# Modulation weights in three chunks instead of four, the last two by narrow strips, with the dummy products on a built-in constant

## The chip, the cores and the metric

The kernel runs on one core of a Trainium2 chip. The metric is the device time of one execution in microseconds (us), and the number that counts is the median of several runs. A profiled execution of the same program, taken by the hardware profiler, gives the trace that the prediction reads.

## What is computed

One block of a two-stream (image and text) transformer with adaptive layer norm: B = 2 batches, 256 image and 32 text tokens each, width D = 1152, all in bfloat16. Cut to the image side, which is what the change touches:

```python
mod = silu(c) @ wmod_img                      # [B, 6*D]; parts 0, 1, 2 are shift, scale, gate
h   = layernorm(x_img) * (1 + scale) + shift
q, k, v = split(h @ wqkv_img)                 # the text side does the same with its own weights
p   = softmax(concat(q_t, q) @ concat(k_t, k).T * D**-0.5)
out = x_img + gate * ((p @ concat(v_t, v)) @ wo_img)
```

## The kernel before, in words

The width of 1152 is KT = 9 blocks of P = 128. The 512 image tokens are four x tiles of 128 rows (tiles 0 and 1 are batch 0, tiles 2 and 3 batch 1). The program is one hand-written order (`manual_schedule`, L62): every engine carries out its instructions in the order of the source, and waits only on semaphores.

**Loads.** All weights come through one queue on SP, in the order of the source. x tiles 0 and 1 go by ACT's queue (L100). On SP there follow the scale weights `w_sc_i` and the value weights `w_v_i` in turn: `KC` (L49) cuts the nine blocks into the chunks 0-1, 2-3, 4-5 and 6-8; `load_sc` (L92) fetches a chunk of scale weights (rows of 512 bytes for two blocks, of 768 bytes for three), `load_v` (L96) the value weights of the same blocks, one block of 288 KB at a time (rows of 2304 bytes). x tile 2 comes behind the first scale chunk, x tile 3 behind value block 6, and then value blocks 7 and 8 in one transfer (L109). After that come the shift weights (`w_sh_i`) and the query weights (`w_q_i`), in thirds.

**Warm-up.** `warm` (L140) issues dummy products of 512 columns on a tile `wz`, which VectorE (DVE) has set to zero (L124): four, then the transpose of `c` and the SiLU (`silu_c`), then eleven more (L312).

**Layer norm and scale.** DVE normalises an x tile into `xn_i` (`stats_of`, `std_of`, `out_of`, L317; the square root is ACT's, L176). TensorE (PE) transposes its blocks: the first H = 2 as "heads" (`x_heads`, L198), which ACT writes out already multiplied by the scale (`head_scaled`, L205), and the others as "tails" (`x_tails`, L210), which are copied out plain (`tail_out`, L217) and multiplied later (`apply_mod`, L251). The scale itself comes in two ways. `mod_scale` (L226) makes it with 9 products of two columns for each block, so 18 for a chunk, and it lands in the layout in which it is used. `mod_scale_last` (L235), used for the last chunk, makes a strip: 4 opening products, 36 products of 96 columns in four column groups of the array, and a 32x32 transpose by DVE (L248) that turns it into columns.

**Values.** `v_row(i, kt)` (L297) multiplies block kt of x tile i with 2 x 512 columns of value weights ("wide" products, L282), `v_narrow` (L290) with the last 128. Seven accumulators stay open over all nine blocks, so these run block by block as chunks arrive (L346 to L402). x tile 3 comes last: `last_transposes` (L301) makes all nine blocks, DVE multiplies them by the scale, and `v_wide(3, ...)` follows. Then comes a strip for the shift (`mod_strip`, L429) and, from L534 on, the query products (L529) and the rest of the block.

Of the kernel before, what the change touches and what calls it, by code (L numbers as in the profile page):

```python
# [8 lines left out]
ACT = mybir.ActivationFunctionType  # L9
# [5 lines left out]
def kernel(  # L15
# [14 lines left out]
    nc = tc.nc  # L30
# [6 lines left out]
    P = 128  # L37
# [8 lines left out]
    SCALE = float(D) ** -0.5  # L46
    EPS = 1e-5

    KC = [(0, 2), (2, 4), (4, 6), (6, KT)]  # L49
    VW = 512  # L50
    NM = 1024

# [52 lines left out]
    for ch in range(1, len(KC)):  # L105
        load_sc(ch)
        if ch < len(KC) - 1:
            load_v(ch)
    for k0, k1 in ((6, 7), (7, KT)):  # L109
        nc.sync.dma_start(w_v_i[:, k0:k1, :], w_view(wqkv_img)[:, k0:k1, 2 * D:3 * D])  # L110
        if k1 < KT:
            load_x(3)
    K3 = ((0, 3), (3, 6), (6, KT))
    K2 = ((0, 5), (5, KT))
    w_sh_i = load_w(wmod_img, 0, K3)
# [5 lines left out]
    eps_t = const.tile([P, 1], f32)  # L121
    nc.vector.memset(eps_t[:], EPS)
    nc.gpsimd.memset(x_t[:], 0.0)
    wz = const.tile([P, VW], bf)  # L124
    nc.vector.memset(wz[:], 0.0)  # L125
    sT32 = const.tile([P, KT, 32], bf)
    nc.gpsimd.memset(sT32[:], 0.0)
    ones_full = const.tile([P, B * 32 + 96], bf)
# [8 lines left out]
    sTw = sTw_full[:, 0:KT * NT].rearrange("p (k b t) -> p k b t", k=KT, b=B)  # L137


    def warm(n):  # L140
        for _ in range(n):
            ps = ps_mm.tile([P, VW], f32, tag="mm", name="wps")
            nc.tensor.matmul(ps[:], lhsT=wz[:, 0:P], rhs=wz[:], start=True, stop=True)  # L143

    sT = const.tile([P, KT, B], bf)

# [55 lines left out]
            nc.tensor.transpose(tp[:, kt, :], xn_i[:, i, kt * P:(kt + 1) * P], ident[:])  # L202
        return tp

    def head_scaled(tp, i):  # L205
        for kt in range(H):
            nc.scalar.activation(hT_i[:, kt, i * P:(i + 1) * P], tp[:, kt, :], ACT.Identity,
                                 scale=mod_i[:, kt, i // TPB:i // TPB + 1])

    def x_tails(i):  # L210
        pool, tag = (ps_mm, "mm") if i < TPB else (ps_sm, "sm")
        tp = pool.tile([P, KT - H, P], bf, tag=tag, name="tp")
        for kt in range(H, KT):
            nc.tensor.transpose(tp[:, kt - H, :], xn_i[:, i, kt * P:(kt + 1) * P], ident[:])
        return tp
# [7 lines left out]
                nc.tensor.matmul(out_ps[:, j - j0, :], lhsT=wt[:, kt, j * P:(j + 1) * P], rhs=sT[:, kt, :],  # L223
                                 start=(kt == 0), stop=(kt == KT - 1))

    def mod_scale(ch, eng, pool=ps_sm, tag="sm"):  # L226
        k0, k1 = KC[ch]
        mps = pool.tile([P, KT, B], f32, tag=tag)
        mod_cols(w_sc_i, mps, k0, k1)
        if eng == "dve":  # L230
            nc.vector.tensor_scalar_add(mod_i[:, k0:k1, :], mps[:, 0:k1 - k0, :], 1.0)
        else:
            nc.scalar.activation(mod_i[:, k0:k1, :], mps[:, 0:k1 - k0, :], ACT.Identity, bias=1.0)

    def mod_scale_last():  # L235
        k0, k1 = KC[3]
        n = (k1 - k0) * 32
        gps = ps_sm.tile([P, n], f32, tag="sm", name="sps3")
        for g in range(NGG):
            nc.tensor.matmul(gps[32 * g:32 * g + 32, :], lhsT=unit[:, 0:32], rhs=unit[:, 0:n], start=True, stop=False,  # L240
                             tile_position=(0, 32 * g))
        for kt in range(KT):
            cols = w_sc_i[:, kt, k0 * P:k1 * P].rearrange("p (m g j) -> p g m j", m=k1 - k0, g=NGG)
            for g in range(NGG):
                nc.tensor.matmul(gps[32 * g:32 * g + 32, :], lhsT=sT32[:, kt, :], rhs=cols[:, g],
                                 start=False, stop=(kt == KT - 1), tile_position=(0, 32 * g))
        t = work.tile([P, VC + 32], f32, tag="of", bufs=1, name="scols")[:, 0:n]
        nc.vector.transpose(t, gps[:])  # L248
        scols[0] = t.rearrange("p (k r) -> p k r", r=32)[:, :, 0:B]

    def apply_mod(kt, t0, t1, shift, eng):  # L251
        b = t0 // TPB
        sl = hT_i[:, kt, t0 * P:t1 * P]
        if shift:
            ap = shift_i[:, kt, b:b + 1]
        elif kt >= KC[3][0]:
            ap = scols[0][:, kt - KC[3][0], b:b + 1]
        else:
            ap = mod_i[:, kt, b:b + 1]
        op = ALU.add if shift else ALU.mult  # L260
        if eng == 0:
            nc.vector.tensor_scalar(sl, sl, ap, None, op0=op)
        elif eng == 1:
            if shift:
                nc.gpsimd.tensor_scalar(sl, sl, 1.0, ap, op0=ALU.mult, op1=ALU.add)
            else:
                nc.gpsimd.tensor_scalar(sl, sl, ap, 0.0, op0=ALU.mult, op1=ALU.add)
        elif shift:
            nc.scalar.activation(sl, sl, ACT.Identity, bias=ap, scale=1.0)
        else:  # L270
            nc.scalar.activation(sl, sl, ACT.Identity, scale=ap)
# [37 lines left out]
            nc.vector.tensor_mul(hT_i[:, j0:j1, i * P:(i + 1) * P], tp[:, j0 - k0:j1 - k0, :],  # L309
                                 mod_i[:, j0:j1, b:b + 1].to_broadcast([P, j1 - j0, P]))  # L310

    warm(4)  # L312
    silu_c()
    warm(11)
    lns = {}

    def stats_of(i, k0, k1):  # L317
# [10 lines left out]
    stats_of(1, 0, NCH)  # L328
    std_of(1)
    out_of(0)  # L330
    mod_scale(0, "act")
    out_of(1)
    tails = []
    for i in range(TPB):
        heads = x_heads(i)
        tails.append(x_tails(i))
        head_scaled(heads, i)
    stats_of(2, 0, NCH)
    tail_out(0, tails[0], H, H + 3)
    std_of(2)  # L340
    tail_out(0, tails[0], H + 3, KT)
    tail_out(1, tails[1], H, H + 3, on_vector=True)
    out_of(2, 0, H * P)
    tail_out(1, tails[1], H + 3, KT, on_vector=True)
    out_of(2, H * P, D)
    for kt in range(*KC[0]):  # L346
        for i in range(TPB):
            v_row(i, kt)
    for i in range(TPB):
        v_narrow(i, *KC[0])  # L350
    head2 = x_heads(2)
    mod_scale(1, "dve")
    head_scaled(head2, 2)
    apply_mod(2, 0, 2, False, 0)
    apply_mod(3, 0, 2, False, 1)
    v_wide(2, 0, *KC[0])
    v_narrow(2, *KC[0])
    tail2 = x_tails(2)
    tail_out(2, tail2, H, KT)
    v_wide(2, 1, *KC[0])  # L360
    for kt in range(*KC[1]):
        apply_mod(kt, 2, 3, False, 0)
    for kt in range(*KC[1]):
        for i in range(TPB):
            v_row(i, kt)
    mod_scale(2, "dve")
    for kt in range(*KC[2]):
        apply_mod(kt, 0, 2, False, 0)
        apply_mod(kt, 2, 3, False, 1)
    for kt in range(*KC[1]):  # L370
        v_row(2, kt)
    k0, k1 = KC[2]
    for i in range(3):
        v_row(i, k0)
    for i in range(TPB):
        v_row(i, k0 + 1)
    for i in range(3):
        v_narrow(i, *KC[1])
    mod_scale_last()
    for n, kt in enumerate(range(*KC[3])):  # L380
        apply_mod(kt, 0, 2, False, (0, 1, 2)[n])
        apply_mod(kt, 2, 3, False, (2, 0, 1)[n])
    nc.gpsimd.tensor_copy(mod_i[:, KC[3][0]:KT, :], scols[0])
    v_row(2, k0 + 1)
    for i in range(3):
        v_narrow(i, k0, k1)
    stats_of(3, 0, NCH)
    std_of(3)
    out_of(3)
    k0 = KC[3][0]  # L390
    for i in range(3):
        v_row(i, k0)
        v_narrow(i, k0, k0 + 1)
    for i in range(3):
        for half in range(2):
            v_wide(i, half, k0 + 1, KT)
        v_narrow(i, k0 + 1, KT)
        if i == 1:
            last_transposes(0, KT - 1, ps_sm, "sm")
            last_transposes(KT - 1, KT, ps_mm, "mm")  # L400
    v_wide(3, 0, 0, KT)
    v_narrow(3, 0, KT)  # L402
# [58 lines left out]
    nc.sync.dma_start(x_t[0:P:P // NTT, :], xt_flat[:, :])  # L461
    w_q_t = load_w(wqkv_txt, 0, K2)
    w_k_t = load_w(wqkv_txt, D, K2)
    w_ga_i = load_w(wmod_img, 2 * D, K2, home="V")
    w_v_t = load_w(wqkv_txt, 2 * D, K3)
    w_o_i = load_w(wo_img, 0, K2)
    w_ga_t = load_w(wmod_txt, 2 * D)
# [461 lines left out]
```

## Time and profile before

| | us |
|---|---|
| median of 3 runs (114.64 to 114.8) | 114.69 |
| the profiled execution, its own time | 114.88 |
| its span, first to last instruction | 113.1 |
| PE busy in the span | 108.3 |
| DVE, ACT and POOL busy | 76.1, 36.6, 28.4 |

All times in the views count from the start of the span. The profiled execution took 1.8 us more than its span and 0.19 us more than the median. A line of a timeline has the start, the time from the first start to the last end, the engine, the source line, the operation, output and inputs, the count, and in brackets the idle time before it with what ended it. Products of PE overlap in the pipe, so the pace of a group is read from the start of one group to the start of the next. SPq and ACTq are the issues of transfers on these queues, not the transfers.

### The profile page before, as it was taken

How to read it: one execution, taken by the hardware profiler on the slowest of the kernel's cores; microseconds unless marked ns; L12 is line 12 of the kernel's file. 1: busy time of each engine (PE TensorE's matmuls, PEld its weight loads, DVE VectorE, ACT ScalarE, POOL GpSimd, SP SyncE). 2: the span in 40 equal slices, each digit the busy share in tenths (PEclk: the TensorE clock that was granted, in tenths of full speed). 3: DMA queues.
4: the chain of work that ended last, by engine and by line, in shares of the span. 5: the costliest groups of instructions: out<-in, count | busy, mean ns of one | idle time of the engine just before them, and what ended most of it. 6: DMA issues, size and time to landing. Idle time of an engine off the chain costs nothing.

```text
span 113.1 us, 2863 instructions
## 1 busy us (share of the span) xinstructions
PE 108.3 (96%) x1195; PEld 64.0 (57%) x1204; DVE 76.1 (67%) x151; ACT 36.6 (32%) x83; POOL 28.4 (25%) x65
## 2 busy tenths in 40 slices
PE   5999999999999999999999999999999999999990
PEld 1356655555444444444446558787687556567670
DVE  1699330956399999999999950237666802995971
ACT  4537500372190071740008924025646700001000
POOL 7100120730140000000000060601550470699300
PEclk9999999999999999999999999999999999999998
DMA  3999999999999999999999999999999999994052
GB/s 92 343 333 355 375 375 405 412 411 408 407 412 412 410 411 402 413 410 412 412 411 415 408 405 407 408 392 394 407 411 397 412 408 406 371 375 161 0 191 70
DMA packets 22839, 40.87 MB, mean 361 GB/s; under 512 B 1375, under 2 KB 6635, under 8 KB 22827
## 3 DMA queue, kind: packets, MB, share of 16 engines
q1 hardware_dynamic: 21547, 39.05, 90.4%
q10 hardware_dynamic: 672, 0.77, 2.2%
q0 software_dynamic: 608, 0.88, 2.1%
q8 instruction: 9, 0.15, 0.5%
q14 instruction: 3, 0.02, 0.1%
HBM read 39.36 MB, written 1.34 MB: 360 GB/s over the span
## 4 chain that ended last, share of the span: by engine, by line
PE 80%; DMA 13%; SPq 4%; issue 1%; DVE 0%
PE qkps L529 31%; PE ps L851 16%; DMA w_sc_i<-in_wmod_img_dram 13%; PE va L282 7%; PE aps L759 5%; PE ps L590 4%; PE sps L619 4%; PE gps L429 3%; SPq L98 3%; PE ops L869 2%; PE ps L694 2%; PE van L294 1%; PE gps L824 1%; PE sps L632 1%; PE pk L703 1%
## 5 line engine op out<-in xcount | busy, mean ns | idle before, releaser
L529 PE MATMUL qkps<-hT_i,t 128*128 128x512 bf16 x158 | 35.4, 379 | 0.2
L529 PEld LDWEIGHTS <-t 128*128 128x128 bf16 x162 | 15.6, 98 | 18.7 <-issue 0.4
L491 DVE SCALAR_TENSOR_TENSOR sacc<-w_v_i,mcols,sacc 128x1152 f32<-128x1152 bf16 x16 | 22.7, 1418 | 0.5
L282 PE MATMUL va<-w_v_i,hT_i 128*128 128x512 bf16 x67 | 17.0, 379 | 0.5 <-issue 0.3
L851 PE MATMUL ps<-t,aT 128*128 128x384 bf16 x99 | 16.4, 326 | 0.0
L851 PEld LDWEIGHTS <-aT 128*128 128x128 bf16 x117 | 11.0, 98 | 6.8 <-issue 0.5
L282 PEld LDWEIGHTS <-hT_i 128*128 128x128 bf16 x72 | 6.4, 98 | 6.2 <-issue 0.2
L835 POOL TENSOR_TENSOR w_og<-t,gb 128x384 bf16<-128x384 bf16 x9 | 8.7, 999 | 4.5 <-DMA gb<-mod_scratch 4.5
L857 DVE TENSOR_TENSOR tmp<-ps,gb 128x384 bf16<-128x384 f32 x11 | 6.0, 550 | 5.6 <-DMA gb<-mod_scratch 5.0
L548 POOL TENSOR_SCALAR mod_txt<-mcols 128x18 f32<-128x18 f32 x2 | 0.6, 275 | 32.4 <-DVE mcols L435 32.4
L169 DVE BATCH_NORM_STATS2 stats<-x_i 128x6 f32<-128x384 bf16 x12 | 5.8, 541 | 2.6 <-DMA x_i<-in_x_img_dram 2.6
L143 PE MATMUL wps<-wz 128*128 128x512 bf16 x15 | 6.1, 578 | 1.2 <-DVE wz L125 1.2
L479 ACT ACTIVATE qT<-qkps 128x512 bf16<-128x512 f32 x9 | 4.7, 600 | 6.9 <-PE qkps L529 6.9
L495 ACT CAST shi<-sacc 128x1152 bf16<-128x1152 f32 x2 | 2.3, 1154 | 13.2 <-DVE sacc L491 13.2
L772 DVE TENSOR_SCALAR aT<-aps,sv 128x288 bf16<-128x288 f32 (+2 forms) x11 | 4.3, 455 | 2.0 <-PE aps L759 2.0
L590 PEld LDWEIGHTS <-t 128*128 128x128 bf16 x162 | 5.0, 98 | 0.5
L157 DVE CAST kT<-qkps 128x512 bf16<-128x512 f32 x3 | 2.1, 686 | 4.7 <-PE qkps L529 4.7
L590 PE MATMUL ps<-hT_t,t 128*128 128x64 bf16 x162 | 5.0, 193 | 0.0
L858 DVE TENSOR_TENSOR o<-tmp,x_i 128x384 bf16<-128x384 bf16 x11 | 4.7, 426 | 0.4
L759 PE MATMUL aps<-pT,v_i 128*128 128x288 bf16 (+2 forms) x44 | 4.8, 264 | 0.0
L774 ACT ACTIVATE aT<-aps,sv 128x288 bf16<-128x288 f32 (+2 forms) x11 | 4.0, 468 | 2.1 <-PE aps L759 2.1
L619 PE MATMUL sps<-kT,qT 128*128 128x288 bf16 x36 | 4.6, 286 | 0.0
(160 smaller groups left out, 139.7 us busy)
## 6 DMA issues: line engine op xcount, KB each, us to landing
t<-in_wqkv_img_dram SPq DMA_DIRECT2D x6, 864.0 KB, 13.2
t<-in_wmod_txt_dram SPq DMA_DIRECT2D x2, 2592.0 KB, 17.6
t<-in_wqkv_txt_dram SPq DMA_DIRECT2D x2, 1440.0 KB, 14.2
t<-in_wmod_img_dram SPq DMA_DIRECT2D x3, 864.0 KB, 12.3
t<-in_wqkv_txt_dram SPq DMA_DIRECT2D x3, 864.0 KB, 14.1
t<-in_wo_txt_dram SPq DMA_DIRECT2D x3, 864.0 KB, 15.5
t<-in_wqkv_txt_dram SPq DMA_DIRECT2D x2, 1152.0 KB, 15.0
w_v_i<-in_wqkv_img_dram SPq DMA_DIRECT2D x7, 288.0 KB, 6.9
```

The lines of the kernel that those rows point to most:

```text
L143: nc.tensor.matmul(ps[:], lhsT=wz[:, 0:P], rhs=wz[:], start=True, stop=True)
L169: nc.vector.bn_stats(stats[0:np_, k, :], x_ap[:, k * CH:(k + 1) * CH])
L282: nc.tensor.matmul(ps[:], lhsT=hT_i[:, kt, i * P:(i + 1) * P], rhs=w_v_i[:, kt, half * VW:(half + 1) * VW], start=(kt == 0), stop=(kt == K ...
L479: nc.scalar.mul(out_ap, in_ap, SCALE)
L491: nc.vector.scalar_tensor_tensor(saccs[b][:], w_v_i[:, kt, :], ap, saccs[b][:], op0=ALU.mult, op1=ALU.add)
L529: nc.tensor.matmul(pss[j - j0][:], lhsT=wq[:, kt, j * P:(j + 1) * P], rhs=hT_i[:, kt, :], start=(kt == 0), stop=(kt == KT - 1))
L590: nc.tensor.matmul(ps[:, j - j0, :], lhsT=wq[:, kt, j * P:(j + 1) * P], rhs=hT_t[:, kt, :], start=(kt == 0), stop=(kt == KT - 1))
L619: nc.tensor.matmul(sps[:], lhsT=qkTs[0][:, ft, b, q0:q0 + P], rhs=qkTs[1][:, ft, b, :], start=(ft == 0), stop=(ft == KT - 1))
L759: nc.tensor.matmul(bank[:, off:off + c1 - c0], lhsT=lhsT, rhs=rhs, start=(first[id(bank)] == n), stop=(final[id(bank)] == n))
L835: nc.gpsimd.tensor_mul(w_og[:, dt, 0:CH], w_o_i[:, dt, NG0:D], gb[:, B - 1, NG0:D])
L851: nc.tensor.matmul(ps[:, 0:cw], lhsT=aT[:, dt, t0:t0 + P], rhs=rhs, start=(dt == DTS[0]), stop=(dt == DTS[-1]))
L857: nc.vector.tensor_mul(tmp[:, 0:cw], ps[:, 0:cw], gb[:, b, cs])
```

## The change

The chunks become three of three blocks (so H = 3). The first scale chunk is made by columns in two parts, blocks 0-1 and block 2 (`mod_scale_first`), the other two by strips (`mod_scale`, the former `mod_scale_last`). Value blocks 7 and 8 come in two transfers, and x tile 3 in one of 120 rows and one of 8. The dummy products read the program's constant of ones, so that `wz` and its memset go, and there are 5 and 13 of them. The order of heads, tails and value products is written anew for chunks of three; the tails' PSUM tiles come from the larger pool. The weights of the image gate (`w_ga_i`), which were two transfers, are one.

```diff
-    KC = [(0, 2), (2, 4), (4, 6), (6, KT)]
+    KC = [(0, 3), (3, 6), (6, KT)]
...
-    for k0, k1 in ((6, 7), (7, KT)):
-        nc.sync.dma_start(w_v_i[:, k0:k1, :], w_view(wqkv_img)[:, k0:k1, 2 * D:3 * D])
-        if k1 < KT:
-            load_x(3)
+    for kt in range(*KC[-1]):
+        nc.sync.dma_start(w_v_i[:, kt:kt + 1, :], w_view(wqkv_img)[:, kt:kt + 1, 2 * D:3 * D])
+        if kt == KC[-1][0]:
+            for p0, p1 in ((0, 120), (120, P)):
+                nc.sync.dma_start(x_i[p0:p1, 3, :], xi_t[p0:p1, 3, :])
...
-    nc.vector.memset(wz[:], 0.0)
+    ones_l = nc.const_aps.tensor(1.0, [P, P], bf)
+    ones_r = nc.const_aps.tensor(1.0, [P, VW], bf)
...
-            nc.tensor.matmul(ps[:], lhsT=wz[:, 0:P], rhs=wz[:], start=True, stop=True)
+            nc.tensor.matmul(ps[:], lhsT=ones_l, rhs=ones_r, start=True, stop=True)
...
-    def head_scaled(tp, i):
-        for kt in range(H):
+    def head_scaled(tp, i, k0=0, k1=H):
+        for kt in range(k0, k1):
...
-        pool, tag = (ps_mm, "mm") if i < TPB else (ps_sm, "sm")
-        tp = pool.tile([P, KT - H, P], bf, tag=tag, name="tp")
+        tp = ps_mm.tile([P, KT - H, P], bf, tag="mm", name="tp")
...
+    def mod_scale_first(k0, k1, pool, tag):
         mps = pool.tile([P, KT, B], f32, tag=tag)
         mod_cols(w_sc_i, mps, k0, k1)
...
+        nc.scalar.activation(mod_i[:, k0:k1, :], mps[:, 0:k1 - k0, :], ACT.Identity, bias=1.0)
...
-    def mod_scale_last():
-        k0, k1 = KC[3]
+    def mod_scale(ch):
+        k0, k1 = KC[ch]
...
-        elif kt >= KC[3][0]:
-            ap = scols[0][:, kt - KC[3][0], b:b + 1]
         else:
-            ap = mod_i[:, kt, b:b + 1]
+            ap = scols[kt // H][:, kt % H, b:b + 1]
...
-    warm(4)
+    warm(5)
     silu_c()
-    warm(11)
+    warm(13)
...
-    mod_scale(0, "act")
+    mod_scale_first(0, H - 1, ps_sm, "sm")
     out_of(1)
...
+    heads, tails = [x_heads(0)], [x_tails(0)]
+    head_scaled(heads[0], 0, 0, H - 1)
+    mod_scale_first(H - 1, H, ps_mm, "mm")
+    heads.append(x_heads(1))
+    tails.append(x_tails(1))
+    for i, kt in ((1, 0), (0, H - 1), (1, 1), (1, H - 1)):
+        head_scaled(heads[i], i, kt, kt + 1)
     stats_of(2, 0, NCH)
...
     std_of(2)
...
+    tail_out(1, tails[1], H, 2 * H, on_vector=True)
     out_of(2, 0, H * P)
...
+    tail_out(0, tails[0], H, 2 * H)
+    tail_out(0, tails[0], 2 * H, KT)
+    tail_out(1, tails[1], 2 * H, KT, on_vector=True)
     out_of(2, H * P, D)
...
-    for kt in range(*KC[0]):
+    for kt in range(H - 1):
         for i in range(TPB):
             v_row(i, kt)
+    v_row(0, H - 1)
+    head2 = x_heads(2)
+    head_scaled(head2, 2)
+    v_row(1, H - 1)
     for i in range(TPB):
         v_narrow(i, *KC[0])
+    tail2 = x_tails(2)
+    tail_out(2, tail2, H, 2 * H, on_vector=True)
+    tail_out(2, tail2, 2 * H, KT)
     v_wide(2, 0, *KC[0])
+    mod_scale(1)
+    v_wide(2, 1, *KC[0])
     v_narrow(2, *KC[0])
     for kt in range(*KC[1]):
+        apply_mod(kt, 0, 2, False, 0)
         apply_mod(kt, 2, 3, False, 0)
+    nc.gpsimd.tensor_copy(mod_i[:, H:2 * H, :], scols[1])
     for kt in range(*KC[1]):
         for i in range(TPB):
             v_row(i, kt)
+        if kt + 1 < KC[1][1]:
+            v_row(2, kt)
+    mod_scale(2)
+    for n, kt in enumerate(range(*KC[2])):
+        apply_mod(kt, 0, 2, False, (0, 1, 2)[n])
+        apply_mod(kt, 2, 3, False, (2, 0, 1)[n])
+    nc.gpsimd.tensor_copy(mod_i[:, 2 * H:KT, :], scols[2])
...
+    v_row(2, 2 * H - 1)
     for i in range(3):
         v_narrow(i, *KC[1])
...
+    for i in range(3):
+        v_row(i, KT - 3)
+        v_narrow(i, KT - 3, KT - 2)
+    for i in range(TPB):
+        v_row(i, KT - 2)
+        v_narrow(i, KT - 2, KT - 1)
...
     for i in range(3):
         for half in range(2):
-            v_wide(i, half, k0 + 1, KT)
+            v_wide(i, half, KT - 1 if i < TPB else KT - 2, KT)
...
+        if i == 0:
+            last_transposes(0, KT - 1, ps_sm, "sm")
         if i == 1:
-            last_transposes(0, KT - 1, ps_sm, "sm")
             last_transposes(KT - 1, KT, ps_mm, "mm")
...
-    w_ga_i = load_w(wmod_img, 2 * D, K2, home="V")
+    w_ga_i = load_w(wmod_img, 2 * D, home="V")
```

## The prediction

> **What bounds the kernel now.** I read the chain of work that ended last first, then PE's timeline up to the query products, then the issues of the first transfers, each asked for its own stretch, with the time from issue to landing. The chain, first column the start, second the length:
>
> ```profile
> 1.21 5.34 DMA w_sc_i<-in_wmod_img_dram
> ...
> 9.82 0.43 SPq L98
> ...
> 10.29 8.84 DMA w_sc_i<-in_wmod_img_dram
> ...
> 19.18 0.57 PE sps L245 x36
> ...
> 31.35 10.03 PE qkps L529 x46
> ...
> 79.02 0.01 PE gps L636 x2
> ```
>
> The chain is transfers until 10.29 + 8.84 = 19.13, when the last chunk of scale weights lands, and from the strip at 19.18 on it is PE. At 31.35 the query products begin, and behind that the change touches one transfer only. So the question is when the last strip can begin, and how much PE work stands behind it. PE's timeline shows how near PE itself was to that wait:
>
> ```profile
> 1.22 1.89 PE L143 MATMUL wps<-wz 128*128 128x512 bf16 x4 [1.22 <-DVE wz L125]
> 3.16 4.22 PE L143 MATMUL wps<-wz 128*128 128x512 bf16 x11
> 7.21 0.59 PE L223 MATMUL mps<-sT,w_sc_i 128*128 128x2 bf16 x18
> 7.85 0.29 PE L202 MATMUL tph<-ident,xn_i 128*128 128x128 bf16 x2
> 9.05 1.89 PE L282 MATMUL va<-w_v_i,hT_i 128*128 128x512 bf16 x7
> ...
> 14.99 0.59 PE L223 MATMUL mps<-sT,w_sc_i 128*128 128x2 bf16 x18
> 15.45 3.18 PE L282 MATMUL va<-w_v_i,hT_i 128*128 128x512 bf16 x14
> 18.47 0.50 PE L294 MATMUL van<-w_v_i,hT_i 128*128 128x128 bf16 x6
> 18.89 0.23 PE L240 MATMUL sps<-ones_full 128*32 128x96 bf16 x4
> 19.18 0.57 PE L245 MATMUL sps<-w_sc_i,sT 128*32 128x96 bf16 x36
> 19.90 0.38 PE L282 MATMUL va<-w_v_i,hT_i 128*128 128x512 bf16 x1 [0.16 <-issue]
> 20.12 0.50 PE L294 MATMUL van<-w_v_i,hT_i 128*128 128x128 bf16 x6
> 20.45 0.60 PE L282 MATMUL va<-w_v_i,hT_i 128*128 128x512 bf16 x2
> ...
> 21.87 0.22 PE L294 MATMUL van<-w_v_i,hT_i 128*128 128x128 bf16 x1
> 22.05 1.02 PE L282 MATMUL va<-w_v_i,hT_i 128*128 128x512 bf16 x4
> ```
>
> PE came to the strip at 18.89, opened it, and stood until 19.18: a bound by two things almost at once. From starts to starts the paces are: a wide product (18.47 - 15.45) / 14 = 0.216 us, a narrow one (20.45 - 20.12) / 6 = 0.055 (a transpose has as many columns and is taken at the same), a column product (15.45 - 14.99) / 18 = 0.026. A strip took 19.90 - 18.89 = 1.01 with its wait of at most 0.25, so 0.76 to 1.01 without; I take 0.85.
>
> **The change part by part.** First, when the last chunk lands. The transfers that count below, with the median time from issue to landing at the end of the row:
>
> ```profile
> w_v_i<-in_wqkv_img_dram SPq DMA_DIRECT2D x2, 288.0 KB, 6.1
> w_v_i<-in_wqkv_img_dram SPq DMA_DIRECT2D x1, 288.0 KB, 5.6
> w_v_i<-in_wqkv_img_dram SPq DMA_DIRECT2D x1, 576.0 KB, 8.4
> w_home<-in_wmod_img_dram SPq DMA_DIRECT2D x1, 1152.0 KB, 14.0
> ```
>
> The issues of three of them on SP's queue:
>
> ```profile
> 2.39 0.91 SPq L98 DMA_DIRECT2D w_v_i<-in_wqkv_img_dram  x2
> ...
> 13.58 0.43 SPq L110 DMA_DIRECT2D w_v_i<-in_wqkv_img_dram  x1
> ...
> 59.58 2.48 SPq L76 DMA_DIRECT2D w_home<-in_wmod_img_dram  x2
> ```
>
> And the rates in three stretches in which scale weights moved (stretch, length, busy time and count for PE, PEld, DVE, ACT, POOL, clock, DMA share, GB/s):
>
> ```profile
> 8.40:10.00 1.60, 1.54 (x16) 1.00 (x15) 1.57 (x5) 1.45 (x5) 0.00 (x0) 1.00 1.08 321
> 12.10:13.40 1.30, 1.30 (x14) 0.91 (x14) 0.24 (x1) 0.36 (x1) 0.48 (x1) 1.00 1.16 369
> 15.00:17.00 2.00, 2.00 (x27) 1.17 (x26) 0.77 (x3) 0.00 (x0) 0.74 (x2) 1.00 1.09 371
> ```
>
> Before and after, the same bytes stand ahead of the last scale block. What changes is the row: 1.77 MB of scale weights move in rows of 768 bytes instead of 512. The first two stretches carry rows of 512 bytes at 321 and 369 GB/s, the third 768 at 371. At the mean of the two, 345, the 1.77 MB take 5.13 us; at 371 they take 4.77. That is 0.36 us (0.03 to 0.74 by the two ends; I take the mean, since neither stretch is cleaner than the other). The last chunk would land at 19.13 - 0.36 = 18.77.
>
> Second, when PE gets there. The first chunk is half as large again: 864 KB at 371 GB/s take 2.39 us, 576 KB at 345 took 1.71, so 0.7 more (0.55 to 0.79 by 321 and 369), and it lands at 1.21 + 5.34 + 0.7 = 7.2. The first two value blocks, issued from 2.39 on with 0.46 between them, landed 6.1 us later, near 8.5 and 9.0, and move to about 9.2 and 9.7.
>
> Dummy products first. The weight loads show their pace:
>
> ```profile
> 3.03 0.10 PEld L149 LDWEIGHTS <-c 18*128 18x128 bf16 x1 [0.84 <-DMA c<-in_c_dram]
> 3.16 0.13 PEld L143 LDWEIGHTS <-wz 128*128 128x128 bf16 x2
> ...
> 6.55 0.33 PEld L143 LDWEIGHTS <-wz 128*128 128x128 bf16 x2 [0.28 <-issue]
> ```
>
> From 3.16 to 6.55 eight dummies begin 0.42 us apart (0.427 once under way); the last three of the eleven take (7.21 - 6.55) / 3 = 0.22 each. Without the memset, PE starts at about 0.75 (when the other engines have their first instruction) instead of 1.22. Five dummies end at 2.9, and the transpose of c still waits until 3.03. So the thirteen begin at 3.16 as the eleven did: eight slow ones until 6.55, five fast ones, end at 7.65. That is 0.44 us later than now, and behind the landing at 7.2. An earlier fast pace gives 7.2, by the landing.
>
> From 7.65 on PE has: 18 column products (0.46), 9 transposes (0.50), 9 column products (0.23), 9 transposes (0.50): first value product at 9.34, against 9.05 now. Then in order: 10 wide (2.16), 3 transposes (0.17), 2 wide (0.43), 6 narrow (0.33), 6 transposes (0.33), 3 wide (0.65): 13.41. The new strip (0.85), whose chunk has 288 KB fewer ahead of it than the third chunk of before, which PE used at 14.99 without standing, then 3 wide and 3 narrow (0.81): 15.07. Then 16 wide (3.45): 18.52, and 0.2 for opening the last strip: 18.7. The second strip adds 0.85 where 27 column products go (0.70), so PE's work is no smaller. What PE gains is waits: its first heads stood until 7.85, the next ones until DVE had x tile 1 (8.48 by the rows below), the heads of x tile 2 until 11.04, and other work is now put in these places.
>
> That PE stands nowhere in this stretch is the weak part. The hand-offs behind it:
>
> ```profile
> 7.90 0.58 DVE L182 TENSOR_SCALAR xn_i<-x_i,mv,rstd 128x1152 bf16<-128x1152 bf16 x1
> 8.24 1.25 ACT L207 ACTIVATE hT_i<-tph,mod_img 128x128 bf16<-128x128 bf16 x4 [0.22 <-PE tph L202]
> 10.17 0.29 ACT L176 ACTIVATE rstd<-mv,eps_t 128x1 f32<-128x1 f32 x1 [0.32 <-DVE mv L174]
> 10.70 0.34 DVE L182 TENSOR_SCALAR xn_i<-x_i,mv,rstd 128x256 bf16<-128x256 bf16 x1
> ...
> 20.70 0.55 DVE L169 BATCH_NORM_STATS2 stats<-x_i 128x6 f32<-128x384 bf16 x1
> ```
>
> ACT now has six head products and one more scale write ahead of the square root of x tile 2. By their pace (0.3 each) they run from 8.45 to 10.4; the square root, the reciprocal and the first 384 columns follow to 11.3. PE asks for them at 11.50. The cover is 0.2 us, and what ACT loses beyond it PE loses. Behind ACT's tail copies stand the next heads; PE's three wide products at 12.8 wait for these, with hardly more cover. For the new strip, 0.81 us of PE work and the return to full products cover DVE's transpose and first multiplication: now 2 wide and 6 narrow products (0.76) do, and the product at 20.45 follows without a gap.
>
> SP issues one transfer more (0.43 us, row of 13.58) ahead of the shift weights; its issues run 5.6 to 9 us ahead of the data by the landings above, so no data wait for that.
>
> So the last strip's weights can be multiplied at 18.82 (the landing, plus the 0.05 that lie between landing and product now), not 19.18: **-0.36 us**. Behind it stand 38 wide products as now, but 27 narrow ones instead of 24: **+0.17**. The wait ahead of 22.05 (0.18 from the last narrow product instead of 0.055) is for value blocks 7 and 8, issued at 13.58 and landed 8.4 us later, at 22.0. They now come in two and earlier: **-0.12**. Sum: **-0.31 us**. From there PE's stages follow back to back, and DVE's shift sums start with PE's shift strip, so all of it moves together. The merged gate weights cost nothing: its second part, issued within 0.5 us of 59.58, landed 14.0 us later, 5 us ahead of its first use at 79.02. The memset that goes cost DVE idle time only; POOL's added copy of six columns has no reader before the last transposes. Against the profiled execution's own 114.88 this gives 114.57; that run stands 0.19 above the median, so on the median it is 114.69 - 0.31 = **114.38**.
>
> x tile 3 in 120 and 8 rows I cost at nothing: DVE begins with it only at 20.70, after the scale products. For what comes behind it the price lies between a tenth of a transfer later (288 KB at 371 GB/s are 0.8 us) and a gain, since the rows show a lag in the landings: value block 5, issued at 9.82, landed 5.6 later at 15.4; 864 KB at 371 GB/s take 2.4, so the last chunk was due at 17.8 and landed at 19.13, 1.3 late. I take the middle.
>
> The Trainium skill ("DMA: Bandwidth & Descriptors", Rules for kernel authors) speaks against the split: it advises against two transfers to disjoint partitions, since they share the same engines and serialise. By that rule value blocks 7 and 8 come no earlier, and the sum would be -0.19. No row of before shows such a split.
>
> **The rivals.**
>
> *No gain, the landing stays.* If rows of 512 bytes cost nothing (369 against 371 speaks for it, 321 against), the last chunk lands at 19.1, and the strip starts where it did: +0.17 - 0.12 = +0.05, so 114.74.
>
> *More gain, the lag goes elsewhere.* The last chunk's lag of 1.3 us may fall on another transfer. Then PE's own 18.7 binds, or with a fast start (7.2 instead of 7.65) 18.25: -0.48 to -0.9 with +0.05, so 113.85 to 114.26.
>
> *Slower, the dummies outlast the data.* If the fast pace comes late, thirteen dummies hold PE while the first chunk lies ready. At the slow pace throughout they end at 3.16 + 13 x 0.427 = 8.71; every step behind moves by 1.06, the strip to 19.76, and the time to 114.69 + 0.58 + 0.05 = 115.3. It decides from an end of the dummies at 8.1 on (no gain left), 8.3 for slower by 0.2%. Waits on ACT of more than 0.5 us in sum do the same. The pace at 6.55 speaks against it. The Trainium skill ("TensorE: Matmul & The Clock Gate", Part 1) has the clock released after one busy window of about 3.4 us, and the windows free-running. By that rule products that begin at 0.75 are fast by 7.6 at the latest, the dummies end by 8.2, and this rival would give at most 114.8; the rows here show one start only, and agree (fast 5.4 us after the first product).
>
> **How the numbers follow.** Forecast (-0.2 to -0.55): 0.45. More gain: 0.10. Landing stays, or ACT's waits eat the gain: 0.27. Slower: 0.18. The range takes all but the ends of the last two: 113.9 to 115.0. A measurement of this kernel can tell 0.2% (0.23 us) from no change; the forecast's own range lies mostly beyond it. So faster 0.53, within 0.2% 0.29, slower 0.18.
>
> **What would show it.** After: dummies from 0.75, fast by 6.6, first column products at 7.2 to 7.7; value products from 9.3; first strip near 13.5, second near 18.8 and right behind the landing of the last scale chunk; no wait near 22; query products at 31.0 instead of 31.3. It is wrong if PE stands for ACT or DVE between 11 and 15, if the second strip starts after 19.2, or if the query products start early and the end does not.

## The result, and the profile after

The changed kernel took **115.59 us** (median of 13 runs, 115.06 to 116.26) against 114.75 (13 runs beside them, 114.58 to 115.2): 1.0067 of the time before, 95% interval 1.0048 to 1.0087. The forecast was 114.38, and the range ended at 115.0. It is slower by 0.84 us, with the sign wrong. A ratio here and below is an estimate over all executions, not the quotient of the two medians.

The profiled execution of the changed kernel took 116.26 us (span 114.5), the slowest of the 13. PE's timeline, the rows that answer to those shown of before (7.21, 7.85, 9.05, 19.18, 22.05, 31.29):

```profile
7.97 0.60 PE L224 MATMUL mps<-sT,w_sc_i 128*128 128x2 bf16 x18
9.80 0.34 PE L204 MATMUL tph<-ident,xn_i 128*128 128x128 bf16 x3 [1.22 <-DVE xn_i L184]
...
11.04 2.32 PE L277 MATMUL va<-w_v_i,hT_i 128*128 128x512 bf16 x9
...
16.64 3.63 PE L277 MATMUL va<-w_v_i,hT_i 128*128 128x512 bf16 x16
20.19 0.23 PE L237 MATMUL sps<-ones_full 128*32 128x96 bf16 x4
20.25 0.56 PE L242 MATMUL sps<-w_sc_i,sT 128*32 128x96 bf16 x36
...
24.55 0.22 PE L289 MATMUL van<-w_v_i,hT_i 128*128 128x128 bf16 x1
24.83 0.62 PE L301 MATMUL tp<-ident,xn_i 128*128 128x128 bf16 x8
...
32.62 1.67 PE L521 MATMUL qkps<-hT_i,t 128*128 128x512 bf16 x7
```

The last strip began at 20.25 instead of 19.18, and the query products at 32.62 instead of 31.29. The whole loss lies ahead of them. The chain of work that ended last begins differently:

```profile
1.15 6.18 DMA x_i<-in_x_img_dram
7.35 1.49 DVE stats L171 x3
...
9.16 0.59 DVE xn_i L184
...
9.80 0.34 PE tph L204 x3
```

x tile 1 landed at 7.33 instead of 4.46, DVE did its statistics ahead of the normalising of tile 0, and PE stood for it. That looked like the cause. The last chunk of scale weights had landed at 17.94 here, so this strip waited for PE's earlier work and not for its weights. The windows of 17 to 21 us (in each the last number is GB/s) show a second thing; first the kernel before, then the changed one:

```profile
18.00:19.00 1.00, 1.00 (x13) 0.62 (x12) 0.00 (x0) 0.00 (x0) 0.00 (x0) 1.00 1.05 409
19.00:20.00 1.00, 0.79 (x41) 0.63 (x39) 0.21 (x1) 0.00 (x0) 0.00 (x0) 1.00 1.05 415
```

```profile
18.00:19.00 1.00, 1.00 (x6) 0.43 (x5) 0.00 (x0) 0.00 (x0) 0.00 (x0) 1.00 1.04 267
19.00:20.00 1.00, 1.00 (x6) 0.39 (x4) 0.00 (x0) 0.00 (x0) 0.00 (x0) 1.00 1.04 293
```

The DMA share stays at 1.04, but the bytes fall by a third, while x tile 3 moves in its 120 and 8 rows. Engines that are as busy as before and move less have slower packets: from 17.75 to 19.5 us a packet of 2304 bytes took 93 ns before and 129 in the mean here.

### The profile page after: what moved, and what is told of

Same layout as the page of the kernel before. It is cut to its first block, busy times and chain, and to the rows that moved or that the text cites. A ratio compares the mean times of both kernels' runs of the same rounds, so it can differ in the third digit from the quotient of the medians.

```text
span 114.5 us, 2896 instructions
## 1 busy us (share of the span) xinstructions
PE 108.9 (95%) x1211; PEld 63.8 (56%) x1220; DVE 76.4 (67%) x151; ACT 37.0 (32%) x87; POOL 27.1 (24%) x63
## 4 chain that ended last, share of the span: by engine, by line
PE 85%; DMA 5%; DVE 5%; issue 1%; ACTq 0%; ACT 0%; DVEq 0%
PE qkps L521 31%; PE ps L843 16%; PE va L277 11%; DMA x_i<-in_x_img_dram 5%; PE aps L751 5%; PE ps L582 4%; PE sps L611 4%; PE gps L421 3%; DVE stats L171 3%; PE ops L861 2%; PE ps L686 2%; PE gps L816 1%; DVE xn_i L184 1%; PE van L289 1%; PE sps L624 1%
## 5 line engine op out<-in xcount | busy, mean ns | idle before, releaser
L145 PE MATMUL wps<-const-bfloat16-1.0 128*128 128x512 bf16 x18 | 7.2, 575 | 0.8 <-PEq L905 0.8
L145 PEld LDWEIGHTS <-const-bfloat16-1.0 128*128 128x128 bf16 x18 | 2.3, 135 | 4.3 <-issue 4.0
```

The source lines that it names most:

```text
L145: nc.tensor.matmul(ps[:], lhsT=ones_l, rhs=ones_r, start=True, stop=True)
```

## The experiments

The theories in order of time. **A**: x tile 1 is late, overtaken by the wider first scale chunk. **B**: the new order with its second strip costs PE more. **C**: the dummies. When these did not explain the loss: **D**: the rows of x tile 3, split 120 + 8. **E**: the last transposes, which the change asks for one row group sooner. **F**: the wider first chunk lands later.

| kernel | median, us | ratio to before, 95% | tile 1 landed | last scale chunk landed | last strip's weights | query products |
|---|---|---|---|---|---|---|
| before | 114.69 to 114.85 | 1 | 4.46 | 19.14 | 19.18 | 31.29 |
| changed | 115.59 | 1.0067 (1.0048 to 1.0087) | 7.33 | 17.94 | 20.25 | 32.62 |
| changed, again | 115.65 | 1.0067 (1.0044 to 1.0090) | 6.39 | 18.04 | 19.31 | 31.89 |
| tile 1 ahead | 116.23 | 1.0120 (1.0097 to 1.0142) | 4.36 | 18.95 | 19.33 | 32.05 |
| normalise tile 0 first | 115.66 | 1.0067 (1.0043 to 1.0092) | 4.52 | 19.67 | 19.71 | 32.36 |
| before, new dummies | 114.66 | 0.9992 (0.9975 to 1.0009) | 4.51 | 18.49 | 18.93 | 30.92 |
| tile 3 whole | 115.10 | 1.0042 (1.0018 to 1.0067) | 6.71 | 17.38 | 19.62 | 32.00 |
| before, tile 3 split | 116.64 | 1.0181 (1.0159 to 1.0203) | 4.48 | 19.81 | 19.85 | 32.09 |
| transposes late | 115.44 | 1.0062 (1.0042 to 1.0081) | 4.52 | 19.82 | 19.86 | 32.01 |
| whole and late | 114.62 | 0.9986 (0.9975 to 0.9998) | 4.51 | 18.52 | 18.67 | 30.81 |
| late, 112 + 16 rows | 115.17 | 1.0029 (1.0010 to 1.0048) | 4.55 | 19.32 | 19.36 | 31.62 |
| late, 64 + 64 rows | 115.24 | 1.0048 (1.0032 to 1.0065) | 6.21 | 18.99 | 19.14 | 31.33 |
| whole, late, narrow first | 114.81 | 1.0007 (0.9993 to 1.0020) | 4.46 | 18.95 | 18.99 | 31.14 |
| late, halves by column | 114.55 | 0.9973 (0.9955 to 0.9991) | 4.62 | 18.51 | 18.56 | 30.71 |

The last four columns are of each profiled execution, which may lie above or below its median. A landing is that of the last of the DMA engines. "Late" names the kernel with the last transposes back in their old place, "whole" the one with x tile 3 in one transfer. Line numbers move by one to three with the edits.

### The changed kernel a second time

> The changed kernel once more, for a second profile of it. Theory A (x tile 1 is overtaken in the DMA engines by the wider first scale chunk, DVE takes the statistics of tile 1 ahead of normalising tile 0, and PE's first transposes wait): tile 1 lands later than 4.5 us again, by an amount that varies from run to run, and the first transposes of tile 0 begin 3.0 to 3.4 us behind that landing if it lies behind 5.2; time 115.1 to 116.2. Theory B (the second strip and the new order cost PE more than counted, and the late tile 1 belongs to the one profiled run alone): tile 1 lands near 4.5, first transposes near 8.1, and the loss of 0.8 us lies between 9 and 21 us; time 115.4 to 115.7.

The time came again; the profile did not. The first column products waited for the first chunk (landed at 7.68), the heads stood for 0.53 instead of 1.22, and the last strip began at 19.31, near to before. The execution was still 0.6 longer than that of before, and a wait stood behind the strip:

```profile
7.72 0.60 PE L224 MATMUL mps<-sT,w_sc_i 128*128 128x2 bf16 x18 [0.84 <-DMA w_sc_i<-in_wmod_img_dram]
8.86 0.34 PE L204 MATMUL tph<-ident,xn_i 128*128 128x128 bf16 x3 [0.53 <-DVE xn_i L184]
...
19.31 0.56 PE L242 MATMUL sps<-w_sc_i,sT 128*32 128x96 bf16 x36
...
24.10 0.62 PE L301 MATMUL tp<-ident,xn_i 128*128 128x128 bf16 x8 [0.27 <-DVE xn_i L184]
```

The query products began 0.60 later than in the profile before: 0.13 at the strip, 0.17 for the three narrow products more, 0.43 for the wait ahead of the transposes (from start to start: 24.10 less 23.61 and 0.055 for the narrow product), less 0.13 for the wait ahead of 22.05 that is gone. The last chunk had landed at 18.04, so this strip did not wait for its weights either.

### x tile 1 ahead of the first scale chunk

```diff
-    for i in range(TPB):
-        load_x(i, nc.scalar)
+    load_x(0, nc.scalar)
+    load_x(1)
```

> The changed kernel with x tile 1 on SP's queue ahead of the first scale chunk instead of on ACT's queue beside it, so that the chunk can't overtake it. Theory A: tile 1 lands by 4.8 us, the first transposes begin near 8.1, the last strip near 18.8, and the time is 114.2 to 114.7, 0.9 to 1.4 below the changed kernel. Theory B: the time stays at 115.4 or more.

Tile 1 landed at 4.36, and the time rose to 116.23. The first chunk, now behind it, landed at 8.38, and the heads began at 8.89, no earlier than in the second profile (8.86). Of the rise of 0.6, nearly 0.5 lies behind the start of the query products (82.30 us to the end of the span, against 81.84 in both profiles of the changed kernel); what makes it was not followed. So this cure does not bring the time back, but it trades one delay of the heads for another and doesn't clear A by itself.

### Tile 0 normalised before tile 1's statistics

```diff
-    stats_of(1, 0, NCH)
-    std_of(1)
     out_of(0)
+    stats_of(1, 0, NCH)
+    std_of(1)
     mod_scale_first(0, H - 1, ps_sm, "sm")
```

> The changed kernel with tile 0 normalised on DVE before the statistics of tile 1, so that a late tile 1 holds up only its own transposes. Theory A: first transposes of tile 0 near 8.2, those of tile 1 still 3 us behind its landing; part of the loss comes back, 0.3 to 0.8 us, 114.8 to 115.3. Theory B: no change, 115.4 to 115.7.

No change, 115.66, although the heads began at 8.38 and tile 1 landed at 4.52. Now the strip stood for its own weights, at a landing later than before's 19.14, and the transposes stood again:

```profile
19.18 0.23 PE L237 MATMUL sps<-ones_full 128*32 128x96 bf16 x4
19.71 0.57 PE L242 MATMUL sps<-w_sc_i,sT 128*32 128x96 bf16 x36 [0.30 <-DMA w_sc_i<-in_wmod_img_dram]
...
24.57 0.62 PE L301 MATMUL tp<-ident,xn_i 128*128 128x128 bf16 x8 [0.33 <-DVE xn_i L184]
```

That tells against A as the whole cause: about the same time comes by two ways, by PE when tile 1 is late and by the last chunk when it is not. DVE also waited 0.17 for x tile 3 itself here, which landed at 21.60 instead of 20.57:

```profile
21.62 1.48 DVE L171 BATCH_NORM_STATS2 stats<-x_i 128x6 f32<-128x384 bf16 x3 [0.17 <-DMA x_i<-in_x_img_dram]
```

### Before, with the new dummies alone

```diff
-    wz = const.tile([P, VW], bf)
-    nc.vector.memset(wz[:], 0.0)
...
-            nc.tensor.matmul(ps[:], lhsT=wz[:, 0:P], rhs=wz[:], start=True, stop=True)
+            nc.tensor.matmul(ps[:], lhsT=ones_l, rhs=ones_r, start=True, stop=True)
...
-    warm(4)
+    warm(5)
...
-    warm(11)
+    warm(13)
```

> The kernel before with the change's dummy products alone: 5 and 13 on the constant of ones, no memset. Theory A: the dummies end near 7.7 and PE's first transposes follow at 8.1 instead of 7.85; 0 to 0.25 us slower, 114.7 to 115.0. A third theory, C (the dummies themselves make the loss, by holding PE or by the operand of ones): 115.4 or more.

No difference (0.9975 to 1.0009). The dummies ended before 6.3 here, and PE then waited for DVE, as it does in the kernel before:

```profile
6.26 0.59 PE L224 MATMUL mps<-sT,w_sc_i 128*128 128x2 bf16 x18
7.83 0.29 PE L203 MATMUL tph<-ident,xn_i 128*128 128x128 bf16 x2 [0.98 <-DVE xn_i L183]
```

Theory C fell. B was not borne out either: the strips of the changed kernel took 0.55 us (15.23 to 15.78) and 0.77 (20.19 to 20.96), less than the 0.85 of the prediction.

### x tile 3 in one transfer

```diff
-            for p0, p1 in ((0, 120), (120, P)):
-                nc.sync.dma_start(x_i[p0:p1, 3, :], xi_t[p0:p1, 3, :])
+            load_x(3)
```

> The changed kernel with x tile 3 in one transfer. Theory D (the rows split 120 + 8 slow the stream and bring tile 3 late, and that is most of the loss): the windows 18:21 go back from about 235 to 340 GB/s towards 400 and more, tile 3 lands 0.5 to 1.0 us sooner than the 21.10 of the changed kernel's second profile, the wait of 0.27 ahead of the last transposes goes, and the time falls by 0.25 to 0.5, to 115.15 to 115.4. Theory E (the wait stands because the transposes are asked for before VectorE is through with the strip's columns and tile 3's norm): in that second profile the statistics of tile 3 start at 21.12, right behind VectorE's last scaling of the strip (20.37 + 0.68), so an earlier landing gains 0.05 at most: 115.6, with the stream back at 400 all the same. Theory F (the loss is the wider first scale chunk): 115.6 too.

115.10: 0.5 less than the changed kernel by the medians, a little more than D had, and E had none of it. By the ratios it is 0.3, and their intervals overlap, so this pair alone doesn't fix the size. The stream kept its rate:

```profile
18.00:19.00 1.00, 1.00 (x6) 0.46 (x5) 0.00 (x0) 0.00 (x0) 0.00 (x0) 1.00 1.05 401
19.00:20.00 1.00, 1.00 (x43) 0.53 (x41) 0.00 (x0) 0.00 (x0) 0.00 (x0) 1.00 1.04 410
```

The nine runs spread from 114.47 to 115.86; the profiled one is among the slowest, with tile 1 landed at 6.71 and PE late from the heads (9.18) on, so the gain doesn't show in its strip.

### Before, with tile 3 in 120 and 8 rows

```diff
-            load_x(3)
+            for p0, p1 in ((0, 120), (120, P)):
+                nc.sync.dma_start(x_i[p0:p1, 3, :], xi_t[p0:p1, 3, :])
```

> The kernel before with x tile 3 in 120 and 8 rows and nothing else. Theory D: the stream falls to 235 to 340 GB/s in the windows 18:21, tile 3 lands 0.5 to 0.8 later than 20.57, and since tile 3's norm takes 3.0 from its landing to the last transposes, these start 0.1 to 0.4 behind the 24.00 of before: 114.85 to 115.2. Theory E: the stream falls as well, but the transposes have 0.4 of slack here, so the time is within 0.1 of before, 114.75 to 114.9. Theory F: no difference.

This is the split with nothing else of the change, and it cost **1.85 us**, more than any theory had. The stream fell, and the last strip stood for its weights with PE's work all done:

```profile
19.00:20.00 1.00, 0.24 (x19) 0.15 (x18) 0.00 (x0) 0.00 (x0) 0.00 (x0) 1.00 1.02 279
```

```profile
18.86 0.23 PE L241 MATMUL sps<-ones_full 128*32 128x96 bf16 x4
19.85 0.57 PE L246 MATMUL sps<-w_sc_i,sT 128*32 128x96 bf16 x36 [0.76 <-DMA w_sc_i<-in_wmod_img_dram]
```

PE's query products began 0.80 later than before (32.09), and its last output products too (105.09 against 104.29). The other 0.96 us lies behind the start of these: to the end of the span it took 9.77 against 8.81. SP's waits in the last stretch, before and then here (us in total, times, the longest):

```profile
SPq L924 <- DMA out_dram<-o: 0.6, 2, 0.4
```

```profile
SPq L925 <- DMA out_dram<-o: 1.1, 1, 1.1
```

SP ends the program by waiting for its transfers' semaphores one after another. With one transfer more, each transfer's semaphore moves on by one: SP's last output stood last of these in the kernel before, and second here, so seven waits (0.5 us) came behind it that had been over by then. The other 0.5 stands in the program's last instructions, from 113.52 to 114.86 here and from 112.25 to 113.10 before; why they took longer no run shows. The changed kernel has as many transfers as the kernel before, 56 against 57 here, and spends 8.84 there, so this part is no part of its loss.

### The last transposes back in their place

```diff
-        if i == 0:
-            last_transposes(0, KT - 1, ps_sm, "sm")
         if i == 1:
+            last_transposes(0, KT - 1, ps_sm, "sm")
             last_transposes(KT - 1, KT, ps_mm, "mm")
```

> The changed kernel with the last transposes of the first eight blocks back behind the second tile's last row group (two wide products and one narrow later, 0.49 of PE work), as before. Theory E: the wait of 0.22 to 0.41 ahead of them goes wholly or nearly so, and the time falls by 0.2 to 0.3, to 115.35 to 115.45. Theory D with tile 3 still late: the wait shrinks by the same 0.2 to 0.3, so this run does not tell D from E by itself; with the run of tile 3 in one transfer it does. Theory F: the wait only moves, 115.6.

115.44, 0.15 to 0.2 less, which the intervals of the ratios don't tell from no change. The wait ahead of the transposes went (24.72, without a bracket), and with tile 1 in time (4.52) the wait that the split makes ahead of the strip stands alone:

```profile
18.64 0.23 PE L237 MATMUL sps<-ones_full 128*32 128x96 bf16 x4
19.86 0.57 PE L242 MATMUL sps<-w_sc_i,sT 128*32 128x96 bf16 x36 [1.00 <-DMA w_sc_i<-in_wmod_img_dram]
...
24.72 0.50 PE L301 MATMUL tp<-ident,xn_i 128*128 128x128 bf16 x6
```

### Both

Tile 3 in one transfer and the last transposes in their old place: the two diffs above together.

> Both: x tile 3 in one transfer and the last transposes where they were before. If the two cure the same wait (D and E): the time of the better of the two alone, 115.35 to 115.45, with 0.6 above before still to be found in the first strip's and the first columns' place. If they add: 115.0 to 115.1. Theory F: 115.6.

**114.62**, less than before (0.9975 to 0.9998) and 1.0 less than the changed kernel. Against the run with the transposes alone, the split is worth 0.82 us. The two do not cure the same wait: the split acts ahead of the strip, the transposes behind it. Together they gave 0.97, apart 0.49 and 0.15; no run says where the other 0.3 comes from. PE now has no gap from 7.76 to the query products:

```profile
18.61 0.23 PE L236 MATMUL sps<-ones_full 128*32 128x96 bf16 x4
18.67 0.56 PE L241 MATMUL sps<-w_sc_i,sT 128*32 128x96 bf16 x36
...
23.51 0.67 PE L300 MATMUL tp<-ident,xn_i 128*128 128x128 bf16 x9
```

Both kernels with tile 3 whole have one transfer less, 55, and took 82.07 us from the start of the query products to the end of the span, against 81.82 with the transposes alone. So the medians put the split about 0.25 too low; ahead of the query products the two profiles differ by 1.20 (32.01 against 30.81).

The packets of this run and of the one before tell what the split does. From 17.75 to 19.5 us, a packet of 2304 bytes took 93 ns here (306 packets, all alike) and 131 in the mean with the split (217 packets); the scale packets of 768 bytes that were still under way took 36 and 49.

### 112 and 16 rows, 64 and 64 rows

Both stand on the kernel with the transposes late, and change one line:

```diff
-            for p0, p1 in ((0, 120), (120, P)):
+            for p0, p1 in ((0, 112), (112, P)):
```

```diff
-            for p0, p1 in ((0, 120), (120, P)):
+            for p0, p1 in ((0, 64), (64, P)):
```

> The changed kernel with the last transposes where they were before, and x tile 3 in 112 and 16 rows instead of 120 and 8 (in 120 and 8 rows: 115.44; in one transfer: 114.62). Theory D1 (the row counts: 120 and 8 rows do not spread evenly over 16 DMA engines, 112 and 16 do): the stream keeps 400 GB/s in the windows 17:20 and the time is 114.6 to 114.8. Theory D2 (any transfer of fewer than all 128 rows slows the others' packets): the stream falls to 230 to 300 GB/s there and the time is 115.2 to 115.5.

> The same with x tile 3 in two halves of 64 rows. Theory D1: no dip, 114.6 to 114.8. Theory D2: a dip at least as long as that of 112 and 16, since both transfers are then part transfers: 115.2 to 115.8. If this one is fast and 112 and 16 is slow, it is neither the count nor the evenness but which rows an engine gets.

D1, the uneven count, fell: both are slow, 115.17 and 115.24. The stream falls as with 120 and 8 (112 and 16 first, then 64 and 64):

```profile
18.00:19.00 1.00, 0.58 (x6) 0.11 (x5) 0.00 (x0) 0.00 (x0) 0.00 (x0) 1.00 1.10 282
```

```profile
18.00:19.00 1.00, 1.00 (x6) 0.30 (x4) 0.00 (x0) 0.00 (x0) 0.00 (x0) 1.00 1.06 248
```

In the halves of 64 rows the packets of 2304 bytes took 139 ns in the mean. Two part transfers instead of one and a small one made the time hardly longer.

### The first two scale blocks by themselves

On the kernel with tile 3 whole and the transposes late:

```diff
-    load_sc(0)
+    load_sc_blocks(0, 2)
     load_x(2)
+    load_sc_blocks(2, 3)
...
-    warm(13)
+    warm(9)
```

> The changed kernel with x tile 3 in one transfer, the last transposes where they were before, the first scale chunk in two transfers (blocks 0 and 1 first as before the change, block 2 behind x tile 2), and 9 dummies instead of 13 in the second group, so that they end before the first blocks land. Theory F (the three-block first chunk, landed 7.72 there against 6.54 before, holds up the first heads by 0.4): the first column products start near 6.6 to 7.0 instead of 7.76, the heads at 7.75 to 7.9 instead of 8.23, the last strip is reached 0.3 to 0.45 sooner unless its own chunk is late, and the time is 114.2 to 114.5. Rival: the block of 256-byte rows takes longer than its share and brings every later chunk 0.2 to 0.4 later, or the last chunk (18.52) ends the wait: 114.6 to 114.9.

The heads came 0.5 sooner (7.72), as F had it, and it brought nothing: 114.81. PE reached the strip at 18.33 and stood until the chunk had landed:

```profile
7.72 0.34 PE L207 MATMUL tph<-ident,xn_i 128*128 128x128 bf16 x3 [0.73 <-DVE xn_i L187]
...
18.33 0.23 PE L240 MATMUL sps<-ones_full 128*32 128x96 bf16 x4
18.99 0.57 PE L245 MATMUL sps<-w_sc_i,sT 128*32 128x96 bf16 x36 [0.43 <-DMA w_sc_i<-in_wmod_img_dram]
```

The rival's time held: the last chunk landed at 18.95 instead of 18.52. That the block in rows of 256 bytes does it is not shown, since 15 of the 16 engines had landed by 17.74, against 17.51 with the wide chunk, and the last engine's landing moves by as much between executions with the same transfers (19.14 in the kernel before, 18.49 with the new dummies).

### Halves by column

On the kernel with the transposes late; both transfers go to all 128 rows:

```diff
-            for p0, p1 in ((0, 120), (120, P)):
-                nc.sync.dma_start(x_i[p0:p1, 3, :], xi_t[p0:p1, 3, :])
+            for c0, c1 in ((0, D // 2), (D // 2, D)):
+                nc.sync.dma_start(x_i[:, 3, c0:c1], xi_t[:, 3, c0:c1])
```

> The changed kernel with the last transposes where they were before, and x tile 3 in two transfers that halve its columns: each goes to all 128 rows, 1152 bytes a row. In one transfer this kernel took 114.62, in halves of 64 rows 115.24, in 112 and 16 rows 115.17, in 120 and 8 rows 115.44. Theory D2 (a transfer to fewer than 128 rows lengthens the packets that move beside it, from 93 to about 140 ns at 2304 bytes): no dip, the windows 18:20 stay near 400 GB/s, the last strip starts at 18.4 to 18.8, 114.6 to 114.8. Rival (one transfer more in the queue is enough): the same dip to 250 to 300 GB/s and 115.1 to 115.5.

**114.55, the fastest version** (0.9955 to 0.9991 of before). Two transfers, as in the changed kernel, and no dip:

```profile
18.00:19.00 1.00, 1.00 (x43) 0.55 (x41) 0.00 (x0) 0.00 (x0) 0.00 (x0) 1.00 1.07 410
```

```profile
18.56 0.57 PE L242 MATMUL sps<-w_sc_i,sT 128*32 128x96 bf16 x36
```

The packets of 1152 bytes took 51 ns and those of 2304 beside them 93. So neither the second transfer nor its issue costs the time: it is that the transfer goes to fewer than 128 rows. This is the cleanest price of the rows: the run with the transposes late has as many transfers, 56, and the same 81.82 us from the query products to the end, and it took 0.89 more by the medians (115.44 against 114.55), 1.0 by the ratios. The lead of 0.07 over one transfer is less than the 0.25 that that kernel loses at its end, so it is no merit of the columns.

## Why the prediction was wrong, point by point

**The step that failed: "x tile 3 in 120 and 8 rows I cost at nothing."** It put nothing for the tile's own reader, DVE, since that came late, and for what comes behind the tile at most a tenth of a transfer, 0.08 us. What moves beside the tile was not asked. The split lengthens the packets under way, the last scale chunk's stragglers among them: with the transposes late its last engine landed at 19.82 instead of 18.52, ahead of the strip, and PE stood for 1.00. It costs 0.82 to 0.89 us by the runs with the transposes late, 0.80 ahead of the query products in the kernel before, and 0.3 to 0.5 in the changed kernel's own order, where the intervals overlap. The own reader was not quite free of it either: in two profiles DVE waited 0.17 and 0.22 for a tile that came at 21.60 and 21.26. The Trainium skill ("DMA: Bandwidth & Descriptors", Rules for kernel authors) advises against two transfers to disjoint partition halves, since they serialise. The advice pointed the right way; what the runs show is another cost, that of the packets beside them. The prediction priced the rule at 0.12 us, on value blocks 7 and 8 alone, which was far too little.

In the two profiles of the changed kernel itself the strip waited for PE and not for its weights, as told above. So the split's price is shown by the exchanged kernels, and how the loss of 0.84 is shared between the split, the transposes and the late x tile 1 over the thirteen executions stays open.

**A step that was left out: the last transposes.** The diff moves them one row group ahead, and the prediction counted the products behind the strip without their place. DVE took 4.5 to 4.9 us from the strip to the end of tile 3's norm (24.04 - 19.31 = 4.73 in the changed kernel's second profile), and PE now comes for it after about 4.4 (in the first profile the transposes would have followed at 24.61, 0.055 behind the narrow product: 24.61 - 20.25) instead of 4.8 (24.00 - 19.18 before). From start to start the wait is 0.22 to 0.57 us in the five profiles with this order; the medians give 0.15 to 0.2 with the split, which the noise may hide, and 0.5 without. The part of this 0.5 that the wait does not cover lies within the spread of the runs with tile 3 whole.

**The last scale chunk, -0.36: borne out in kind, its size not settled.** The packets took 27 ns for 512 bytes and 36 for 768. The 1.77 MB were 3456 rows, over 16 engines 216 x 27 ns = 5.83 us, and are 2304 rows, 144 x 36 = 5.18: -0.65, an estimate that takes an engine's packets one behind the other. The landings don't confirm that much. The last engine landed at 18.52 and 18.51 without the split, against 19.14, but also at 18.49 in the kernel before with the new dummies, whose transfers are those of before. The 19.13 of the sum belongs to one execution. On 15 of the 16 engines the chunk had landed by 17.69 and 17.83 with the old chunks and by 17.51 and 17.37 with the new ones, 0.2 to 0.5 sooner. The prediction's stretches of 321, 369 and 371 GB/s mixed rows of 2304 bytes with both.

**The first chunk at 7.2, the first value product at 9.34.** It landed at 7.45 to 7.93 where nothing was put ahead of it, and the first value product began at 9.2 to 9.5 where tile 1 was in time and DVE's order unchanged. Later than meant, and of no consequence: the narrow first chunk showed that the strip then waits for its weights.

**Dummies until 7.65, and no stand of PE between 11 and 15**: the dummies ended between 6.6 and 8.0 in the runs with thirteen of them in the changed order, and the column products began within 0.05 us of the chunk's landing in all but one (0.23 behind it, at 7.80, with the transposes late). PE's timelines of the changed kernel show no stand in that stretch. The fast pace of before came 5.33 us after the first product (6.55 - 1.22), not 5.4, which changes nothing in the sum. **The three narrow products, +0.17**: nine took 21.68 - 21.18 = 0.50 and six 0.33, as costed. **The wait ahead of 22.05**: gone, as forecast, but it is gone too in the kernel before with the new dummies, where the product follows at 21.67 behind 21.61. So the change is not shown to be what ended it. **The merged gate weights**: no run tried them alone.

**The rivals.** None was this one. The slower rival was the dummies, which a run of their own cleared in the kernel before. The signs named beforehand did speak: the second strip came after 19.2, in the first profile and in the second.

Without the split and with the transposes in their place, the change does give about what was forecast: -0.27% with the halves by column, 0.31 us, between 0.1 and 0.5 (0.19 by the medians, 114.74 and 114.55). That the number is the same is partly luck: two terms of the sum, -0.36 and -0.12, were read from waits of one execution that another with the same transfers did not have, and PE itself opened the strip only at 18.45 and 18.61.

What stays open: in four profiles x tile 1 landed at 6.2 to 7.3 instead of 4.4 to 4.6, with the same transfers in the same order in three of them as in runs where it was early. The five other profiles with the wide first chunk beside it, and the four with a narrow first chunk, do not show it. No run settled why.

## What to carry to other kernels

Cost a transfer by what it does to the transfers beside it, not only by when its own reader comes: here a 288 KB tile with a late reader cost 0.8 to 0.9 us because it slowed the bytes that were wanted next. If a tile must be split, try columns first and keep all 128 rows: here that cost nothing that the runs can tell. Don't build a sum on one execution's landing. Where an order is rewritten, list every instruction that moved relative to the engine that feeds it, and read packet times, not mixed GB/s, for the worth of a row's length.

## What the runs showed of the hardware

While the transfers to 64, 112 or 120 rows moved, the packets under way were slower in the mean: 2304 bytes took 125 to 148 ns in the eight profiles with such a split (packets from 17.75 to 19.5 us), single ones over 200, against 93 to 95 in the six without. The Trainium skill ("DMA: Bandwidth & Descriptors", The descriptor swizzle) says that in a transfer to 128 partitions each engine writes rows that belong to one port of its own. If a transfer to fewer rows gives the engines other rows, several of them may meet at one port. That is an inference. The packet times agree with it, at 93 and 51 ns for all 128 rows and more for the three splits by rows; the ports themselves no run shows.

The last engine's landing trails the others. With halves by column the last scale chunk had landed on 15 engines by 17.37 us and on the last one at 18.51; in the kernel before it was 17.69 and 19.14. A 16 KB packet of instructions starts near 16 us in both of these traces and takes 0.95 us, on a queue of its own in the page of the profile (packets, MB, share):

```profile
q8 instruction: 9, 0.15, 0.5%
```

That this packet holds up the one engine is not shown. With tile 3 whole it starts at 15.78 in one profile, where the last engine trails by 1.0, and at 16.92 in the other, where it trails by 0.2. With the split one starts at 16.90 and the lag is 2.1, so the packet's start alone does not set it. This is the lag that the prediction saw in the landings and could not place.
